# Transposing q and k of two more batches by the DMA crossbar instead of TensorE, with two crossbar target buffers

## The chip, the cores and the metric

The kernel runs on one core of a Trainium2 chip. The metric is the device time of one execution in microseconds (us). All times below are from executions on the chip. Each kernel was also profiled once; positions such as "at 70.2" are microseconds from the start of that profiled execution. Experiments were timed in rounds that alternate with the kernel before on the same chip. A run that is over 1.5% above the fastest of the same kernel is called slow and left out of the ratios; the others are called fast. "Granted clock" is the clock that the profile shows for TensorE, as a share of full speed. A "crossbar transpose" is a DMA that transposes what it moves (`dma_start_transpose`); PSUM is the memory that TensorE writes its results to.

## The reference

Windowed attention over 8 batches of 8 heads, 576 positions of width 64, followed by a two-layer network with a squared ReLU. Inputs and outputs are float32; the kernel computes in bfloat16.

```python
scores = scale * np.matmul(q, k.transpose(0, 1, 3, 2))        # (8, 8, 576, 576)
mask_plain = (rel >= 0) & (rel < 32)                           # heads 0 to 3
mask_dil = (rel >= 0) & (rel < 32 * 4) & (rel % 4 == 0)        # heads 4 to 7
...
attn = softmax(masked scores)
x = (attn @ v), heads joined                                   # (4608, 512)
h = np.maximum(x @ w_in, 0.0)                                  # (4608, 2048)
out = (h * h @ w_out)                                          # (4608, 512)
```

## The kernel before

The instruction order is written by hand in a string. Batches are numbered from 0, so the "third" batch is 2 and the "fourth" is 3. A "|" ends one group of feed-forward matmuls (288 groups in all, about 0.87 us of TensorE each); the codes between two bars are attention steps put behind that group. `2q0` puts q of head pair 0 of batch 2 into `qT`, `2k0` does the same for k; capital `Q` and `K` are the second part of a batch whose sequence is handled in two parts; `a` and `b` are the two halves of the scores with their exponential, `o` and `p` the two halves of the products with v; `v` spreads v. `L2:q...` loads q and k of batch 2, `L2:v...` loads v, and `L4:x` issues the four crossbar transposes of batch 4, a "quartet" in the order k, q, k, q.

```python
XB = 4                          # batches from here on go through the crossbar
WHOLE = tuple(range(2, XB))     # batches 2 and 3: loaded in one piece, transposed on TensorE
ADDED = 4
ps_f = ...tile_pool(name="ps_f", bufs=4, space=PSUM)   # feed-forward sums
ps_a = ...tile_pool(name="ps_a", bufs=2, space=PSUM)   # "pa": transposes AND scores
rb = [{nm: const.tile([80, 2 * H * RES * D], bf16, ...) for nm in "qk"} for i in range(2)]
qx = const.tile([P, H, 2, M], bf16, name="qx")         # crossbar targets, one of each
kx = const.tile([P, H, 2, M], bf16, name="kx")

def cross(b, nm, part):                                # one crossbar transpose, in SP's queue
    n, m0 = MN[part], MS[part]
    nc.sync.dma_start_transpose(
        (qx if nm == "q" else kx)[:, :, :, m0 : m0 + n].rearrange("p h c m -> p (h c) m"),
        staged(b, nm)[0:n, part, :, :].rearrange("p h x -> p (h x)"),
    )

def trans(b, e, nm, part):                             # transposes on TensorE
    ps = ps_a.tile([P, 1024], bf16, name="pa")
    copy = nc.scalar.copy if nm == "q" and e < NE // 2 else nc.vector.tensor_copy
    ...
    if b in WHOLE:
        m0, n, pitch, cuts = 0, M, M, [(t[0:72, :, a, :], 72 * a, 72) for a in range(2)]
    else:
        m0, n, pitch, cuts = MS[part], MN[part], 80, [(t[0:80, part, :, :], 0, 80)]
    pv_ = ps[:, 0 : 4 * pitch].rearrange("p (h c m) -> p h c m", h=2, c=2)
    for hl in range(2):
        for c in range(2):
            for src, c0, w in cuts:
                nc.tensor.transpose(pv_[:, hl, c, c0 : c0 + w],
                                    src[:, 2 * e + hl, P * c : P * c + P], ident[0:w, 0:w])
    halves(e, nm, pv_[:, :, :, 0:n], m0, n, copy)      # copies into qT or kbd

def scores(b, e, part, ...):
    ps = (pool or ps_a).tile([P, 512], f32, name=name) # the same two "pa" buffers
    ...                                                # matmuls kbd x qT
    nc.scalar.activation(pt[:, off : off + n], ps[:, 0:n], ACT.Exp, scale=SCALE)
    ...                                                # mask on VectorE

def step(b, code):
    ...
    if what in "qk" and b >= XB:                       # crossbar target to qT or kbd
        t = qx if what == "q" else kx
        halves(e, what, t[:, 2 * e : 2 * e + 2, :, :], 0, M, nc.vector.tensor_copy)
    elif what in "qQkK":
        trans(b, e, what.lower(), part)
...
def cross_all(b):
    for part in range(2):
        for nm in "kq":
            cross(b, nm, part)
```

All loads are issued by GpSimd in program order, and all output stores and crossbar transposes by SP in program order.

The softmax here doesn't subtract the row's maximum and nothing guards it: scores larger than these inputs give would overflow.

Of the kernel before, what the change touches and what calls it, by code (L numbers as in the profile page):

```python
# [12 lines left out]
RES = 4  # L13
# [5 lines left out]


PROGRAM = (
    "L0:q023 L0:q00 L0:q01 0k0 L0:q10123 0q0 0q1 0k1 L0:v0pd 0a0 0q2 L0:i0 0a1 0k3 L0:v1dpr 0k2 0q3 0Q1 "
    "0K3 0a3 0Q3 0K2 0a2 0v2 0Q0 L0:i1 L0:o2 0K0 0o0 0v3 0b0 0Q2 0o2 0K1 0b3 0o1 L0:o0 0o3 0V3 0b2 0b1 | "
    "0V2 | 0p0 | 0p1 0p2 | L0:o1 0p3 L0:o3 | | | y | | | | | | | | L1:q00123 z | | | | | L1:v0dp "
    "L1:q10123 | | L2:qw0123 L1:v1dpr 1q1 1q3 | 1q2 | 1k2 | 1k1 1v3 | 1a2 | 1v2 1k0 1q0 | 1o2 | 1a0 1a1 | "
    "1k3 1o0 1o1 | 1a3 1Q0 | 1K0 1o3 | 1Q1 1K1 | 1Q2 | 1b0 | | 1Q3 1K2 L2:vwpdr | | | 2q0 | | 2k0 1V2 | "
    "1b2 1p0 | 1b1 1V3 1K3 | | 1p2 1p1 | 2a0 1b3 | 2k1 2o0 2b0 1p3 | 2q1 2k2 | | L3:qw0123 2q2 2p0 "
    "L3:vwpdr 2a1 | | | 2b1 | 2v2 2o1 2q3 2a2 | | 2p1 | 2k3 | 2b2 2o2 | 2v3 | 2a3 2p2 L4:q10123 | 2b3 | "
    "3k1 2o3 3q1 | | 3a1 L4:q00123 2p3 | 3k0 3k2 | | 3o1 | | | 3q0 3v2 | | | | 3a0 | 3b1 3k3 | | | 3p1 "
    "L4:x 3q2 | | 3b0 | 3a2 3q3 3o0 4k0 | | | 3o2 3b2 | | 3p0 3v3 | 4q1 3a3 | 3p2 4q2 4q0 | L5:q10123 3b3 "  # L30
    "| 3o3 L4:vwpdr | 4k1 | | L5:q00123 3p3 4k2 4k3 4a0 L5:vwpdr | | | 4b0 | | 4q3 | | 4o0 | | | 4a2 4v2 "
    "| 4b2 | 4a3 L5:x 4a1 | 4o2 | | | 4p2 L6:q00123 4v3 | | 4b1 | | 4p0 | | 4p1 | 5q0 5k0 | 4b3 | | | | "
    "4o1 | | 5k2 L6:q10123 4o3 | 5q2 5k1 | | 4p3 | 5q1 |"
)


# [24 lines left out]
def kernel(  # L61
# [9 lines left out]
    nc = tc.nc  # L71
    P = nc.NUM_PARTITIONS
    B, H, S, D = q.shape
# [3 lines left out]
    bf16 = mybir.dt.bfloat16  # L77
# [11 lines left out]
    MN = (64, M - 64)  # L89
    NT = 512  # L90
    NTILES = NTOK // NT
    XB = 4
    WHOLE = tuple(range(2, XB))
    PARTED = (0, 1)
    ADDED = 4
    RING = 4 * S
# [33 lines left out]
    rb = [{nm: const.tile([80, 2 * H * RES * D], bf16, name=f"{nm}b{i}") for nm in "qk"} for i in range(2)]  # L130
    qT = const.tile([P, NE, RES, M], bf16, name="qT")

    qx = const.tile([P, H, 2, M], bf16, name="qx")
    kx = const.tile([P, H, 2, M], bf16, name="kx")
    kbd = const.tile([P, NE, NB, P], bf16, name="kbd")
    vbd = [const.tile([P, NE, NB, P], bf16, name=f"vbd{i}") for i in range(2)]

# [5 lines left out]
    def staged(b: int, nm: str):  # L143


        t = rb[b % 2][nm]
        if b in WHOLE:
            return t[:, :].rearrange("p (h a x) -> p h a x", h=H, a=2)
        return t[:, :].rearrange("p (a h x) -> p a h x", h=H, a=2)

    def load_qk(b: int, part, es):
        hs = slice(2 * es[0], 2 * es[-1] + 2)
        for nm, src in (("q", q), ("k", k)):
            t = staged(b, nm)
            if b in WHOLE:
                nc.gpsimd.dma_start(
                    t[0 : M // 2, hs, :, :].rearrange("p h a x -> p (h a) x"),
                    src[b, hs, :, :].rearrange("h (a p r) d -> p (h a) (r d)", a=2, r=RES),
                )
            else:  # L160
                t0, n = RES * MS[part], MN[part]
                nc.gpsimd.dma_start(  # L162
                    t[0:n, part, hs, :], src[b, hs, t0 : t0 + RES * n, :].rearrange("h (p r) d -> p h (r d)", r=RES)
                )

    def load_v(b: int, parts, which="pdr"):

# [46 lines left out]
    def cross(b: int, nm: str, part: int):  # L214

        n, m0 = MN[part], MS[part]
        nc.sync.dma_start_transpose(
            (qx if nm == "q" else kx)[:, :, :, m0 : m0 + n].rearrange("p h c m -> p (h c) m"),
            staged(b, nm)[0:n, part, :, :].rearrange("p h x -> p (h x)"),
        )  # L220

    def trans(b: int, e: int, nm: str, part: int):

        ps = ps_a.tile([P, 1024], bf16, name="pa")
        t = staged(b, nm)
        copy = nc.scalar.copy if nm == "q" and e < NE // 2 else nc.vector.tensor_copy
        if b == 0:

            m0, n = MS[part], MN[part]
            pv_ = ps[:, 0 : RES * n].rearrange("p (r m) -> p r m", r=RES)  # L230
            for r in range(RES):
                for hl in range(2):
                    nc.tensor.transpose(  # L233
                        pv_[64 * hl : 64 * hl + 64, r, :],
                        t[0:n, part, 2 * e + hl, D * r : D * r + D],
                        ident[0:n, 0:n],
                    )
            if nm == "q":
                copy(qT[:, e, :, m0 : m0 + n], pv_)
                return  # L240
            for hl in range(2):
                rows = slice(64 * hl, 64 * hl + 64)
                if e < NE // 2:
                    copy(  # L244
                        kbd[rows, e, m0 // 16 : (m0 + n) // 16, rows].rearrange("p i (m r) -> p i m r", r=RES),
                        pv_[rows, :, :].rearrange("p r (i m) -> p i m r", m=16),
                    )
                else:
                    copy(kbd[rows, e, RES * part : RES * part + RES, rows], pv_[rows, :, 0:64])  # L249
                    if part:  # L250
                        copy(
                            kbd[rows, e, 8, rows].rearrange("p (m r) -> p m r", r=RES),
                            pv_[rows, :, 64:n].rearrange("p r m -> p m r"),
                        )
            return
        if b in WHOLE:
            m0, n, pitch, cuts = 0, M, M, [(t[0:72, :, a, :], 72 * a, 72) for a in range(2)]
        else:

            m0, n, pitch, cuts = MS[part], MN[part], 80, [(t[0:80, part, :, :], 0, 80)]  # L260
        pv_ = ps[:, 0 : 4 * pitch].rearrange("p (h c m) -> p h c m", h=2, c=2)
        for hl in range(2):
            for c in range(2):
                for src, c0, w in cuts:
                    nc.tensor.transpose(  # L265
                        pv_[:, hl, c, c0 : c0 + w], src[:, 2 * e + hl, P * c : P * c + P], ident[0:w, 0:w]
                    )
        halves(e, nm, pv_[:, :, :, 0:n], m0, n, copy)

    def halves(e: int, nm: str, t, m0: int, n: int, copy):  # L270


        for hl in range(2):
            rows = slice(64 * hl, 64 * hl + 64)
            for jj in range(2):
                src = t[64 * jj : 64 * jj + 64, hl, :, :]
                if nm == "q":
                    copy(  # L278
                        qT[rows, e, :, m0 : m0 + n].rearrange("p (c j) m -> p j c m", j=2)[:, jj, :, :], src
                    )  # L280
                elif e < NE // 2:
                    copy(  # L282
                        kbd[rows, e, m0 // 16 : (m0 + n) // 16, rows].rearrange(
                            "p i (m c j) -> p j i m c", c=2, j=2)[:, jj, :, :, :],
                        src.rearrange("p c (i m) -> p i m c", m=16),
                    )
                else:
                    x0, x1 = m0 // 64, min((m0 + n) // 64, 2)
                    copy(
                        kbd[rows, e, RES * x0 : RES * x1, rows].rearrange(  # L290
                            "p (x c j) m -> p j c x m", c=2, j=2)[:, jj, :, :, :],
                        src[:, :, 0 : 64 * (x1 - x0)].rearrange("p c (x m) -> p c x m", m=64),
                    )
                    if m0 + n == M:
                        copy(
                            kbd[rows, e, 8, rows].rearrange("p (m c j) -> p j m c", c=2, j=2)[:, jj, :, :],
                            src[:, :, n - 16 : n].rearrange("p c m -> p m c"),
                        )
# [163 lines left out]
    def step(b: int, code: str):  # L462



        what, e = code[0], int(code[1])
        part = int(what in "QKVbp")
        if what in "qk" and b >= XB:
            t = qx if what == "q" else kx
            halves(e, what, t[:, 2 * e : 2 * e + 2, :, :], 0, M, nc.vector.tensor_copy)  # L470
        elif what in "qQkK":
            trans(b, e, what.lower(), part)
        elif what in "vV":
            spread_v(b, e, [part] if b in PARTED else [0, 1])
        elif what in "ab":
            scores(b, e, part, *((ps_f, "pf") if b == 0 and not part else ()))
        elif b == 0 and part and e % 2:
            pv(b, e, part, ps_a, "pa")
        elif b in PARTED and e % 2:
            pv(b, e, part, ps_f, "pf")  # L480
        else:
            pv(b, e, part)
# [224 lines left out]
```

## Time and profile before

| | before |
|---|---|
| time, median of 4 runs (lowest to highest) | 319.07 us (318.94 to 319.78) |
| span of the profiled execution | 317.3 us |
| TensorE busy, granted clock | 94%, 1.000 |
| VectorE, ScalarE, GpSimd busy | 66%, 62%, 27% |

The prediction below shows the page's main lines. In the trace the columns are start, duration, engine, source line, operation, written and read tiles, shapes and count; a bracket at the end, where there is one, is the idle time before the group and what ended it.

```profile
70.50 0.39 PE L334 MATMUL pa<-qT,kbd 128*128 128x32 bf16 x6
70.72 0.31 PE L265 MATMUL pa<-mk,kb 80*128 80x80 bf16 x4
71.08 1.67 PE L561 MATMUL pf<-w_out_sb,h2T 128*128 128x512 bf16 x7
72.59 0.44 PE L443 MATMUL po<-pt,vbd 128*128 128x32 bf16 x9
```

The row at 70.72 is `1K3`, four transposes of the second batch, which stay on TensorE after the change. Like the scores at 70.50 they write a "pa" buffer. There are only two of those, so `1K3` can't start until ScalarE has read the scores that used the buffer before. Here there is no bracket: nothing waits.

SP's queue while a quartet runs with little beside it (batch 4):

```profile
100.13 1.34 SPq L217 DMA_TRANSPOSE kx<-kb  x1
101.65 1.76 SPq L217 DMA_TRANSPOSE qx<-qb  x1
103.52 1.99 SPq L217 DMA_TRANSPOSE kx<-kb  x1
105.61 1.97 SPq L217 DMA_TRANSPOSE qx<-qb  x1
```

The duration here is the time SP needs to issue the transpose, 1.3 to 2.0 us each. The last one lands at 110.02, 9.9 us after the first was issued.

### The profile page before, as it was taken

Reading aid. Unit: us, or ns where it says so; the run is one execution under the profiler, and the core shown is the slowest. Engines: PE = TensorE matmul, PEld = TensorE weight load, DVE = VectorE, ACT = ScalarE, POOL = GpSimd, SP = SyncE. Lnnn points to the kernel's source line nnn. Section 1 sums busy time; section 2 is a strip of 40 time slices with the busy share of each in tenths; the row PEclk is TensorE's granted clock in tenths of the full one; section 3 lists DMA queues with packets and bytes.
Section 4 is the critical chain, followed back from the end, with each engine's and each line's share of the span. In section 5 each row is a group of like instructions: output and inputs, shape, how many; then the busy total and the mean of one; then the engine's idle time right before and its main releaser. Section 6 shows DMA issues by size and latency. Waiting matters only on the chain.

```text
span 317.3 us, 6743 instructions
## 1 busy us (share of the span) xinstructions
PE 299.7 (94%) x2523; PEld 190.3 (60%) x2556; DVE 208.6 (66%) x664; ACT 195.4 (62%) x422; POOL 84.1 (27%) x130
## 2 busy tenths in 40 slices
PE   1698999999999999999999999999999999999995
PEld 1587945877965555555579755555555555445543
DVE  6785758898987987996599658965896324204400
ACT  5366735877958966686468646864686466316511
POOL 8762282367320037741271041000000000000000
PEclk9999999999999999999999999999999999999999
DMA  7999999999996619999699864352200210021022
GB/s 96 179 123 212 207 144 204 130 91 162 108 119 130 120 16 204 159 186 167 91 132 174 134 99 90 49 103 68 66 2 2 68 66 0 24 78 33 0 68 66
DMA packets 73056, 33.08 MB, mean 104 GB/s; under 512 B 44096, under 2 KB 67008, under 8 KB 73024
## 3 DMA queue, kind: packets, MB, share of 16 engines
q0 software_dynamic: 48096, 18.36, 50.3%
q1 hardware_dynamic: 24784, 14.16, 19.0%
q8 instruction: 20, 0.33, 0.4%
q10 hardware_dynamic: 144, 0.13, 0.1%
q14 instruction: 12, 0.10, 0.1%
HBM read 36.83 MB, written 9.44 MB: 146 GB/s over the span
## 4 chain that ended last, share of the span: by engine, by line
PE 88%; DVE 5%; ACT 3%; issue 2%; DMA 1%; POOL 1%; ACTq 0%; DVEq 0%; POOLq 0%
PE pf L529 38%; PE pf L561 37%; PE po L443 3%; PE pd L445 3%; PE pa L265 2%; PE pa L334 2%; PE pa L340 1%; DMA kb<-in_k_dram 1%; DVE xT L458 1%; PE pa L233 1%; DVE kbd L244 1%; DVE kbd L249 1%; ACT rec L447 1%; ACT qT L278 1%; ACT rec L448 1%
## 5 line engine op out<-in xcount | busy, mean ns | idle before, releaser
L529 PE MATMUL pf<-xT,w_in 128*128 128x256 bf16 (+1 forms) x758 | 132.9, 325 | 1.2 <-DVE xT L458 0.3
L561 PE MATMUL pf<-w_out_sb,h2T 128*128 128x512 bf16 (+1 forms) x569 | 131.0, 373 | 1.7 <-ACT osb L567 0.5
L529 PEld LDWEIGHTS <-w_in 128*128 128x128 bf16 x768 | 82.1, 114 | 35.7 <-issue 1.3
L540 ACT ACTIVATE h2T<-pf 128x512 bf16<-128x512 f32 x144 | 83.4, 597 | 24.7 <-PE pf L529 23.8
L561 PEld LDWEIGHTS <-h2T 128*128 128x128 bf16 x592 | 54.2, 98 | 53.5 <-issue 0.7
L541 DVE TENSOR_TENSOR h2T<-h2T 128x512 bf16<-128x512 bf16 x144 | 57.3, 422 | 36.0 <-ACT h2T L540 34.8
L567 ACT COPY osb<-pf 128x512 f32<-128x512 f32 (+1 forms) x37 | 21.2, 573 | 44.5 <-PE pf L561 41.5
L458 DVE TENSOR_TENSOR xT<-po,rec 128x288 bf16<-128x288 f32 (+2 forms) x56 | 25.5, 456 | 34.8 <-ACT rec L448 34.2
L447 ACT ACTIVATE rec<-pd 128x288 f32<-128x288 f32 (+2 forms) x56 | 23.1, 412 | 28.1 <-PE pd L445 28.0
L179 POOL DMA_DIRECT2D vbd<-in_v_dram x40 | 28.2, 728 | 43.8 <-PE pd L445 34.6
L344 ACT ACTIVATE pt<-pa 128x352 bf16<-128x352 f32 (+6 forms) x60 | 29.7, 502 | 8.4 <-PE pa L340 4.4
L448 ACT ACTIVATE rec<-rec 128x256 f32<-128x256 f32 (+2 forms) x64 | 28.4, 444 | 2.0
L443 PEld LDWEIGHTS <-vbd 128*128 128x128 bf16 x332 | 19.6, 99 | 10.2 <-issue 1.4
L443 PE MATMUL po<-pt,vbd 128*128 128x32 bf16 (+3 forms) x286 | 19.6, 199 | 0.7 <-DVE xT L458 0.7
L445 PE MATMUL pd<-pt,mk 128*128 128x96 bf16 (+5 forms) x172 | 18.0, 207 | 0.0
L162 POOL DMA_DIRECT2D qb<-in_q_dram x14 | 10.1, 721 | 27.0 <-PE po L443 24.6
L192 POOL DMA_DIRECT2D vd<-in_v_dram x24 | 14.7, 648 | 9.6 <-DMA kb<-in_k_dram 9.6
L278 DVE COPY qT<-qx 64x288 bf16<-64x288 bf16 x64 | 16.1, 251 | 0.8
L282 DVE COPY kbd<-kx 64x288 bf16<-64x288 bf16 x32 | 15.0, 469 | 0.4
L198 POOL DMA_DIRECT2D vbd<-in_v_dram x16 | 9.7, 617 | 17.4 <-PE pd L445 5.1
L334 PE MATMUL pa<-qT,kbd 128*128 128x96 bf16 (+2 forms) x160 | 13.8, 206 | 0.5 <-DVE kbd L244 0.4
L445 PEld LDWEIGHTS <-mk 128*128 128x128 bf16 x232 | 13.7, 99 | 0.7 <-issue 0.5
(60 smaller groups left out, 231.0 us busy)
## 6 DMA issues: line engine op xcount, KB each, us to landing
out_dram<-osb SPq DMA_DIRECT2D x18, 128.0 KB, 4.8
vd<-in_v_dram POOLq DMA_DIRECT2D x32, 64.0 KB, 5.2
w_in<-in_moe_w_in_dram POOLq DMA_DIRECT2D x2, 1024.0 KB, 9.0
w_out_sb<-in_moe_w_out_dram POOLq DMA_DIRECT2D x4, 512.0 KB, 13.5
qb<-in_q_dram POOLq DMA_DIRECT2D x6, 320.0 KB, 5.1
kb<-in_k_dram POOLq DMA_DIRECT2D x6, 320.0 KB, 6.6
vbd<-in_v_dram POOLq DMA_DIRECT2D x24, 72.0 KB, 5.8
out_dram<-osb SPq DMA_DIRECT2D x10, 160.0 KB, 2.2
```

What stands on the lines that cost most here:

```text
L179: nc.gpsimd.dma_start(dst[rows, e, i0:i1, rows], v[b, 2 * e + hl, 64 * i0 : 64 * i1, :].rearrange("(i p) d -> p i d", p=64),)
L344: nc.scalar.activation(pt[:, off : off + n], ps[:, 0:n], ACT.Exp, scale=SCALE)
L443: nc.tensor.matmul(oo, vb[:, e, i, :], rh, start=(x == 0), stop=(x == len(mms) - 1), skip_group_check=True)
L445: nc.tensor.matmul(dd, ones[:, :], rh, start=(x == 0), stop=(x == len(dms) - 1), skip_group_check=True)
L447: nc.scalar.activation(rec[:, 0:n], d[:, 0:n], ACT.Ln)
L448: nc.scalar.activation(rec[:, 0:n], rec[:, 0:n], ACT.Exp, scale=-1.0)
L458: nc.vector.tensor_tensor(out=tok, in0=o if o is o3 else o[:, 0:n], in1=rec if o is o3 else rec[:, 0:n], op=ALU.mult)
L529: nc.tensor.matmul(acc[u][:, nt * x + y0 : nt * x + y1], w_in_sb[piece][:, kt, c0 : c0 + 509 : 4], xT[:, kt, t0 : t0 + y1 - y0], start=(kt ...
L540: nc.scalar.activation(hv, acc[u][:, :].rearrange("p (x n) -> p x n", x=per), ACT.Relu)
L541: nc.vector.tensor_tensor(out=hv, in0=hv, in1=hv, op=ALU.mult)
L561: nc.tensor.matmul(cur[m][:, c0:c1], h2[:, f, P * m : P * m + P], w_out_sb[:, f, c0:c1], start=(f == 0), stop=(f == NF - 1),)
L567: nc.scalar.copy(osb[:, c0:c1], cur[m][:, c0:c1])
```

## The change

The intent is to take 128 transposes off TensorE, the engine that bounds the kernel, by giving them to the crossbar, which the later batches use already. A second pair of target buffers lets a quartet start while the one before is still being copied out. The order string gets `L2:x` and `L3:x`, and the first readers of batch 3 move two groups later.

```diff
-  ... L2:qw0123 ... 1Q2 | 1b0 | ... L3:qw0123 2q2 2p0 ... 2p1 | 2k3 ...
+  ... L2:q00123 L2:q10123 ... 1Q2 L2:x | 1b0 | ... L3:q00123 L3:q10123 2q2 2p0 ... 2p1 L3:x | 2k3 ...
-  ... 2b3 | 3k1 2o3 3q1 | | 3a1 L4:q00123 2p3 | 3k0 3k2 ...
+  ... 2b3 | 2o3 | | 3k1 3q1 L4:q00123 2p3 | 3a1 3k0 3k2 ...
-    XB = 4
-    WHOLE = tuple(range(2, XB))
+    XB = 2
-    qx = const.tile([P, H, 2, M], bf16, name="qx")
-    kx = const.tile([P, H, 2, M], bf16, name="kx")
+    qx = [const.tile([P, H, 2, M], bf16, name=f"qx{i}") for i in range(2)]
+    kx = [const.tile([P, H, 2, M], bf16, name=f"kx{i}") for i in range(2)]
 (the branches for WHOLE in staged, load_qk and trans go; cross writes qx[b % 2] or kx[b % 2])
-            t = qx if what == "q" else kx
-            halves(e, what, t[:, 2 * e : 2 * e + 2, :, :], 0, M, nc.vector.tensor_copy)
+            t = (qx if what == "q" else kx)[b % 2]
+            by_act = what == "q" and e < NE // 2 and b < ADDED
+            halves(e, what, t[:, 2 * e : 2 * e + 2, :, :], 0, M, nc.scalar.copy if by_act else nc.vector.tensor_copy)
```

## The prediction

> **What bounds the kernel now.** I read the page from the top: the engine shares, then the 40 slices, then the chain that ended last.
>
> ```profile
> PE 299.7 (94%) x2523; PEld 190.3 (60%) x2556; DVE 208.6 (66%) x664; ACT 195.4 (62%) x422; POOL 84.1 (27%) x130
> ...
> PE   1698999999999999999999999999999999999995
> ...
> PE 88%; DVE 5%; ACT 3%; issue 2%; DMA 1%; POOL 1%; ACTq 0%; DVEq 0%; POOLq 0%
> ```
>
> TensorE (PE) is 94% busy over the whole span. The slices show that the missing part is the first 30 us and the last slice; from there on every slice is 9, and the chain of waits lies on PE for 88%. So an instruction taken from PE between 30 and 313 us is worth what it occupies there, as long as no new wait opens. A table of stretches of 10 us shows the neighbours in the stage that is changed: PE 9.95, 9.89 and 9.90 of 10 in the stretches from 60 to 90 us, VectorE 9.29, 8.88 and 9.46, ScalarE 7.31, 8.11 and 8.01. PE is full, VectorE nearly so.
>
> The transposes that go are one line of the kernel. The groups by shape show the 128 that concern the third and fourth batch (72 rows each; the 64 of 80 rows belong to the second batch and stay):
>
> ```profile
> L265 PE MATMUL pa<-mk,qb 72*128 72x72 bf16 x64 | 3.4, 196 | 0.0
> L265 PE MATMUL pa<-mk,kb 72*128 72x72 bf16 x64 | 3.2, 197 | 0.0
> ```
>
> The columns are busy us, mean ns, idle us before. The 6.6 us of busy time is the union of overlapping instructions with pipelined tails; what a group takes away from the next one is read in the order of time on PE:
>
> ```profile
> 67.78 0.42 PE L265 MATMUL pa<-mk,kb 72*128 72x72 bf16 x8
> 68.04 1.03 PE L561 MATMUL pf<-w_out_sb,h2T 128*128 128x512 bf16 x4
> ```
>
> Eight transposes start at 67.78 and the next feed-forward matmul starts at 68.04: 0.26 us for eight, although the group is "busy" 0.42. The other groups of eight with a complete record have the same 0.26.
>
> **What the Trainium skill says.** "VectorE: DVE Perf Modes", section "The three transpose paths", gives 390 ns for a 128x128 transpose on TensorE and 1309 ns by the crossbar. The trace does not bear out the first as a cost: one lasts 196 ns, and in a row they come every 32 ns (0.26/8). "DMA: Bandwidth & Descriptors", section "DMA Transpose (X-bar)", puts the plain transpose on SP or ACT alone; the kernel issues all on SP, in one row with the output stores, so they wait for one another. The same page, "Issuing engines are not separate DMA queues", says that loads, stores and transposes share the same 16 engines and interleave. The trace agrees: the four transposes of one batch land within 9.9 us when little else moves (issued from 100.13 to 105.61, about 4.4 us each to landing), but took from 133.78 to about 150.8 us (144.97 plus a landing of 5.8) while the loads of q and k of a later batch were under way, though part of that is a wait on the single target buffer. "Rules for kernel authors" of the page advises to issue a DMA early and wait for it late; this is the weak point below.
>
> **The change part by part.**
>
> Removed from PE: for each of two batches, q and k, four head pairs, 2 x 2 x 2 pieces = 128 transposes in 16 groups of eight. 16 x 0.26 = **4.2 us**, all on PE in the full stretch from 65.8 to 115.7 us, so on the path.
>
> Removed from PSUM: 16 uses of the two "pa" buffers that the scores share. PE idled 0.5 us in total from 60 to 120 us (10 minus the busy time of each stretch), so at most some 0.3 us are to be had here.
>
> Copies: the same 128-partition halves are copied, now from SBUF. VectorE: q 304 to about 235 ns (from the rows of later batches), 16 of them, 1.1 us; k of the dilated heads 287 to 225 ns, 16, 1.0 us; k of the plain heads 480 to 469 ns, 16, 0.2 us. VectorE gets 2.3 us freer, off the path. ScalarE keeps its 16 copies of q at 391 ns; its mask copies from SBUF of the same width take 431 ns, so it may lose 0.6 us, off the path too.
>
> Added: eight transposing DMAs, four per batch, 1.15 MB per batch, no engine time but SP's queue. Loads of q and k of these batches become four DMAs instead of two, with the same bytes; GpSimd issues at about 0.7 us instead of 1.03, so 0.8 us more per batch, off the path.
>
> Second target buffer: it takes away the wait that held one transpose of the sixth batch from 133.78 to 137.29. Nothing on PE waited for it then (PE is 9.95 of 10 busy there), so no gain is counted.
>
> So far: -4.2 to -4.5 us. Now the **new wait**. The third batch's four transposes come in SP's order after nine stores; the ninth is issued at about 59.6 us (three stores from 58.32, together 1.26). The loads they need were issued at 43.3 and 44.3 and landed after 10.6 and 14.7 us, so at 53.9 and 59.0; both are there. From 59.6 the unhindered quartet lands its last part, q, at 59.6 + 9.9 = 69.5. But the first reader of that q is on ScalarE:
>
> ```profile
> 65.84 0.60 ACT L540 ACTIVATE h2T<-pf 128x512 bf16<-128x512 f32 x1 [0.28 <-PE pf L529]
> 66.33 1.60 ACT L278 COPY qT<-pa 64x288 bf16<-64x288 bf16 x4
> 69.38 0.60 ACT L344 ACTIVATE pt<-pa 128x512 bf16<-128x512 f32 x1 [1.46 <-PE pa L334]
> 69.88 0.43 ACT L447 ACTIVATE rec<-pd 128x320 f32<-128x320 f32 x1
> 70.34 0.47 ACT L448 ACTIVATE rec<-rec 128x320 f32<-128x320 f32 x1
> 70.72 0.57 ACT L567 COPY osb<-pf 128x512 f32<-128x512 f32 x1
> 71.19 0.57 ACT L344 ACTIVATE pt<-pa 128x480 bf16<-128x480 f32 x1
> ```
>
> The order of instructions leaves these copies where they were, at 66.3. ScalarE would stand until q lands, L, and everything behind it shifts: copies to L+1.8, exponential to L+2.4, reciprocals to L+3.3, the output copy to L+3.85, the second exponential to L+4.4, its mask on VectorE to L+4.85. PE needs that last one for the second of two products that now start at 72.59 and 73.09; with two groups of transposes gone it would be there at 72.57. Hence a stall of L - 67.7: 1.8 us for L = 69.5, and it eats the whole gain at L = 71.9.
>
> What L will be: the v loads of the third batch are issued from 60.9 to 67.5 and run beside the quartet. In the stretch 174 to 178 v loads and transposes ran side by side at 218 GB/s in all, so I put 1 to 1.5 us on it: L = 70.5 to 71. From about 69.5 the fourth batch's q and k loads start (now three of them at once), and in 138 to 144 such loads nearly stopped the transposes; if the last one is still under way then, L goes to 75 or 76. I chose a stall of 3 us as central. The fourth batch's quartet comes after stores at 77.0 and its loads' landing (83.9 at the latest, now), and its first reader is moved two groups later, to about 95; I count 0.2 us.
>
> Sum: 319.1 - 4.3 + 3.0 + 0.2 = 318.0; I state 317.8, since the tuning of the program around the new reads suggests that the change was meant to gain.
>
> **The rivals.**
>
> First, the transfer is hidden: q lands by 69.5 or ScalarE's delay is absorbed by the run of feed-forward matmuls that needs no ScalarE. For it: the copies stand at the start of such a run (eight groups from 66.05). Against it: two products of the second batch sit inside that run and need ScalarE. It would give 319.1 - 4.5 + 1 = 315.6.
>
> Second, the wait takes the place of what was removed and more: L at 75 to 76 gives a stall of 7.5 to 8, so 319.1 - 4.3 + 7.8 = 322.6. For it: the starved transposes of 138 to 144. Against it: the quartet starts ten us before those loads.
>
> Third, VectorE becomes the bound from 60 to 90, once PE gets through faster: it is at 9.46 of 10 at most and loses 2.3 us of work over the two batches against 4.2 on PE, so at most some 0.5 us.
>
> **Range and chances.** The best case, 4.5 us gained with no stall, is 314.6, which is 1.4% below 319.08: a gain over 2% (312.7) would need more than the transposes occupy. A loss over 2% (325.5) would need a stall of 10.7 us. So within 2% is nearly sure. The range 315.0 to 321.8 runs from an almost hidden quartet to a stall of 7 us. Chances: faster 0.01, within 2% 0.96, slower 0.03.
>
> **What would show it.** No 72-row transposes on PE; the groups of feed-forward matmuls at 67.8 to 68.9 closing up by 0.26 us each. A wait of ScalarE for the transposing DMA of q at about 66, of 3 to 5 us, and right after it PE idle for some 3 us at about 72 before the second batch's products, released by VectorE or ScalarE. If PE shows no idle time there, the first rival is right; if ScalarE waits 9 us or more, the second. The prediction is wrong if PE stalls elsewhere, for instance behind output stores held up by the transposes in SP's queue, or behind the fourth batch's copies at about 95.

## The result and the profile after

The kernel after takes 328.93 us (median of 4 runs, 327.2 to 332.05), against 319.07 us before. The ratio is 1.031, with a 95% interval of 1.026 to 1.037: slower by 3.1%. A ratio in this document is the mean time of one kernel's fast runs over that of the other's of the same rounds, so it is not quite the ratio of the quoted medians. All four runs count as fast; the granted clock is 0.979 to 0.984 in each, against 1.000 before, and that turns out to be part of the story. Results are correct here and in every experiment.

From the page of the kernel after: busy shares, TensorE in 40 slices (8.2 us each), the clock granted to it, and the engine shares of the chain that ended last.

```profile
PE 299.9 (92%) x2428; PEld 187.1 (57%) x2428; DVE 206.8 (63%) x664; ACT 195.5 (60%) x422; POOL 85.6 (26%) x134
...
PE   1698999963999799999999999999999999999995
...
PEclk9999999995999999999999999999999999999999
...
PE 67%; DMA 21%; POOL 5%; SPq 3%; issue 2%; ACT 2%; DVE 0%; ACTq 0%; POOLq 0%
```

A hole of 6 and 3 stands in the ninth and tenth slices of TensorE, a shallow one follows at the fourteenth, and the clock falls to 5 in the tenth. DMA, 1% of the chain before, is 21% of it now; 5% of the span are transposes of q, and 11% are loads of v, most of them before the hole. Although 128 transposes have gone, TensorE's busy time has not fallen. Part of that is bookkeeping: 33 feed-forward matmuls are missing from the records of before (758 and 569 in its two groups, where the kernel after has 768 and 592). The other part is work done at half clock.

The order of time on TensorE around the hole:

```profile
65.80 2.75 PE L550 MATMUL pf<-w_out_sb,h2T 128*128 128x512 bf16 x12
...
69.98 0.39 PE L320 MATMUL pa<-qT,kbd 128*128 128x32 bf16 x6
78.49 0.42 PE L251 MATMUL pa<-mk,kb 80*128 80x80 bf16 x4 [8.12 <-ACT pt L330]
78.71 3.62 PE L550 MATMUL pf<-w_out_sb,h2T 128*128 128x512 bf16 x8
```

At 65.80 the feed-forward matmuls run through where two groups of transposes had stood. The scores that started at 70.50 before start at 69.98 now, so 0.52 us have been gained by two groups of eight. Then `1K3` waits 8.12 us for an exponential on ScalarE (line 330) to free a "pa" buffer. After the wait, eight matmuls take 3.62 us.

ScalarE shows what the exponential itself waited for:

```profile
66.00 0.60 ACT L529 ACTIVATE h2T<-pf 128x512 bf16<-128x512 f32 x1 [0.28 <-PE pf L518]
76.06 1.75 ACT L264 COPY qT<-qx 64x288 bf16<-64x288 bf16 x4 [9.46 <-DMA qx<-qb]
77.84 0.60 ACT L330 ACTIVATE pt<-pa 128x512 bf16<-128x512 f32 x1
```

The copies of q for the third batch, at 66.33 before, stand until the crossbar transpose of q has landed, 9.46 us. The exponential comes after them in ScalarE's order, though it has nothing to do with that q. SP's queue and a table of stretches of the same time (length; busy us and instructions of TensorE, weight loads, VectorE, ScalarE, GpSimd; granted clock; DMA packets' time as a multiple of the 16 engines' time; GB/s):

```profile
60.47 1.35 SPq L208 DMA_TRANSPOSE kx<-kb  x1
62.00 1.99 SPq L208 DMA_TRANSPOSE qx<-qb  x1
64.09 3.88 SPq L208 DMA_TRANSPOSE kx<-kb  x1
68.07 3.14 SPq L208 DMA_TRANSPOSE qx<-qb  x1
```

```profile
64.00:68.00 4.00, 4.00 (x30) 2.81 (x28) 3.71 (x17) 2.05 (x4) 2.49 (x5) 1.00 1.81 96
```

```profile
72.00:73.00 1.00, 0.00 (x0) 0.00 (x0) 0.00 (x0) 0.00 (x0) 0.00 (x0) 0.95 1.31 244
73.00:74.00 1.00, 0.00 (x0) 0.00 (x0) 0.80 (x2) 0.00 (x0) 0.00 (x0) 0.50 1.44 223
74.00:83.00 9.00, 4.51 (x25) 2.20 (x25) 4.51 (x18) 4.06 (x9) 2.21 (x3) 0.50 0.82 104
83.00:84.00 1.00, 1.00 (x18) 0.76 (x16) 0.00 (x0) 0.75 (x2) 0.27 (x1) 0.93 1.48 260
```

The third transpose takes 3.88 us to issue and the fourth 3.14, where the free quartet took under 2. The four land at 66.37, 70.82, 73.05 and 75.98: 15.5 us from the first issue to the last landing, against 9.9 us when little else moves. While the v loads of the third batch and the quartet share the DMA engines (64 to 68), only 96 GB/s move. The clock reads 0.95 over the microsecond from 72 and 0.93 over that from 83, with 0.50 between, so it was halved for 0.10 + 10 + 0.14 = 10.24 us, from 72.9 to 83.14. TensorE works again from 78.49, so 4.65 us of work ran at half speed and about 2.3 us were lost.

The fourth batch's quartet is issued at 87.66, 90.14, 91.74 and 99.28, beside loads of the fifth batch's q and k issued from 88.70 to 90.84, and lands at 95.25, 102.98, 106.27 and 107.26. TensorE waits in four pieces: 0.36 us at 89.43, 0.35 at 97.16, 0.80 at 109.14 and 1.08 at 110.55, 2.6 us in all. Only the last two, 1.9 us, can be put down to the fourth batch. The first two are waits for products that VectorE scales (`xT`), and such a pair (0.33 and 0.34, 0.29 and 0.34) also stands in the two experiments below that send the third batch alone through the crossbar, and not in those with the fourth alone. So they come with the third batch, late quartet or not.

The balance of the two profiled spans, 326.6 against 317.3, so +9.3 us:

| term | us |
|---|---|
| transposes gone, 16 x 0.26 | -4.2 |
| idle before `1K3` | +8.1 |
| two short waits that come with the third batch | +0.7 |
| two waits for the fourth batch | +1.9 |
| work at half clock, 78.49 to 83.14 | +2.3 |
| start-up of this execution | +0.2 |
| sum | +9.0 |

The remaining 0.3 us are not assigned.

### The profile page after: what moved, and what is told of

It is laid out like the page before. It is cut to its first block, busy times and chain, and to the rows that moved or that the text cites. A ratio compares the mean times of both kernels' runs of the same rounds, so it can differ in the third digit from the quotient of the medians.

```text
span 326.6 us, 6546 instructions
## 1 busy us (share of the span) xinstructions
PE 299.9 (92%) x2428; PEld 187.1 (57%) x2428; DVE 206.8 (63%) x664; ACT 195.5 (60%) x422; POOL 85.6 (26%) x134
## 4 chain that ended last, share of the span: by engine, by line
PE 67%; DMA 21%; POOL 5%; SPq 3%; issue 2%; ACT 2%; DVE 0%; ACTq 0%; POOLq 0%
PE pf L550 31%; PE pf L518 29%; DMA vd<-in_v_dram 11%; DMA qx<-qb 5%; DMA w_in<-in_moe_w_in_dram 3%; SPq L208 3%; PE po L429 2%; PE pd L431 2%; DMA qb<-in_q_dram 2%; PE pa L320 1%; POOL kb L153 1%; POOL vbd L170 1%; POOL qb L153 1%; PE pa L326 1%; ACT qT L264 1%
## 5 line engine op out<-in xcount | busy, mean ns | idle before, releaser
L550 PE MATMUL pf<-w_out_sb,h2T 128*128 128x512 bf16 (+1 forms) x592 | 136.2, 377 | 0.5 <-ACT osb L556 0.5
L170 POOL DMA_DIRECT2D vbd<-in_v_dram x40 | 28.2, 722 | 61.3 <-PE pd L431 46.4
L268 DVE COPY kbd<-kx 64x288 bf16<-64x288 bf16 x48 | 22.6, 471 | 6.0 <-DMA kx<-kb 5.2
L264 DVE COPY qT<-qx 64x288 bf16<-64x288 bf16 x80 | 20.0, 250 | 1.1
L153 POOL DMA_DIRECT2D qb<-in_q_dram x18 | 13.1, 729 | 22.0 <-DMA qx<-qb 16.2
L153 POOL DMA_DIRECT2D kb<-in_k_dram x18 | 12.9, 718 | 9.8 <-PE pa L251 8.1
```

The lines of the kernel that those rows point to most:

```text
L153: nc.gpsimd.dma_start(t[0:n, part, hs, :], src[b, hs, t0 : t0 + RES * n, :].rearrange("h (p r) d -> p h (r d)", r=RES))
L170: nc.gpsimd.dma_start(dst[rows, e, i0:i1, rows], v[b, 2 * e + hl, 64 * i0 : 64 * i1, :].rearrange("(i p) d -> p i d", p=64),)
L264: copy(qT[rows, e, :, m0 : m0 + n].rearrange("p (c j) m -> p j c m", j=2)[:, jj, :, :], src)
L550: nc.tensor.matmul(cur[m][:, c0:c1], h2[:, f, P * m : P * m + P], w_out_sb[:, f, c0:c1], start=(f == 0), stop=(f == NF - 1),)
```

## The experiments

The theory: the third batch's q lands late because its quartet shares the DMA engines with the loads that GpSimd has just issued. ScalarE, which takes its instructions in order, stands before that q and holds a PSUM buffer that TensorE needs. The idle time then halves the clock. The rivals: the fourth batch is the cause; the moved readers or the second buffer are; or a crossbar quartet is too slow here in any case.

In experiment kernels that hold loads back, GpSimd copies one column of the quartet's last target, which makes it wait for the quartet. The code is `h` for batch 2 and `i` for batch 3:

```diff
+        if code == "h":
+            nc.gpsimd.tensor_copy(held[:, 0:1], qx[0][:, 0, 0, M - 1 : M])
+        elif code == "i":
+            nc.gpsimd.tensor_copy(held[:, 0:1], qx[1][:, 0, 0, M - 1 : M])
```

The results in one table. L is when q of the third batch landed, "wait at `1K3`" is TensorE's idle time there, and "half clock" is the length of the stretches at clock 0.5, all from the profiled execution.

| kernel | median us | ratio to before (95%) | L | wait at `1K3` | half clock |
|---|---|---|---|---|---|
| after | 328.93 | 1.0312 (1.0257 to 1.0367) | 76.0 | 8.12 | 10.24 |
| fourth batch only | 318.28 | 0.9961 (0.9945 to 0.9976) | none | none | none |
| third batch only | 330.83 | 1.0337 (1.0299 to 1.0374) | 78.5 | 9.69 | 10.24 |
| v loads held | 328.90 | 1.0294 (1.0277 to 1.0310) | 70.5 | 2.16 | 6.83, later |
| unused matmuls in the hole | 331.69 | 1.0227 (1.0171 to 1.0282) | 78.9 | 2.91 | none |
| q, k loads held | 324.82 | 1.0181 (1.0149 to 1.0213) | 73.4 | 5.31 | 6.83 |
| held for both batches | 328.92 | 1.0300 (1.0272 to 1.0329) | 70.6 | 2.03 | 6.83, later |
| fourth only, readers back | 318.72 | 0.9974 (0.9954 to 0.9994) | none | none | none |
| early quartet, both held | 325.34 | 1.0162 (1.0121 to 1.0204) | 67.9 | none | 3.41 twice, later |
| two buffers only | 319.32 | 0.9993 (0.9977 to 1.0009) | none | none | none |
| q, k loads held, matmuls in the hole | 322.48 | 1.0108 (1.0075 to 1.0141) | 72.3 | filled | none |
| early quartet only | 322.04 | 1.0085 (1.0047 to 1.0123) | 71.6 | 3.82 | 3.41 |
| third only, early, v held | 319.23 | 0.9992 (0.9970 to 1.0013) | 68.1 | under 0.3 | none |

The median of "unused matmuls in the hole" is that of all four runs, two of them slow; its ratio is that of the two fast ones. The medians of before in the same rounds were 319.31 us (first four experiments), 319.48 (next four) and 319.69 (last four).

### Each batch by itself

Only the fourth batch goes through the crossbar; the third is loaded and transposed as before. The two buffers and the later readers stay.

```diff
-    XB = 2          # order: L2:q00123 L2:q10123 ... 1Q2 L2:x
+    WHOLE = (2,)    # order: L2:qw0123 ... 1Q2
```

> Only the fourth batch goes through the crossbar; the third stays on the array as before. Theory A (the loss is the third batch's wait: its q lands at 76 us because loads starve the quartet, and ScalarE, then TensorE stand for it): without that quartet no 8 us wait and no halved clock; 8 groups of 8 transposes less, -2.1 us, so about 317.0 us, granted clock 1.00; the fourth batch's quartet has some 10 us of slack. Rival B (any crossbar batch beside these loads costs): the fourth batch's wait, 2.1 us of PE idle near 108 us in the changed kernel, stays or grows: 319 to 321 us.

Measured: 318.28 us, 0.4% faster than before, 1.3 us above what was expected. Its largest wait on TensorE is one of 0.61 us at 99.95, and the clock stays at 1. Its quartet is issued at 78.0 to 85.2, some ten us earlier than in the kernel after because nothing has held the program up, and lands by 92.7.

The reverse, only the third batch, with the order of before for the fourth:

```diff
-    XB = 2          # order: L3:q00123 L3:q10123 ... 2p1 L3:x ... 2o3 | | 3k1 3q1 ... | 3a1
+    WHOLE = (3,)    # order: L3:qw0123 ... 2p1 ... 3k1 2o3 3q1 | | 3a1
```

> Only the third batch goes through the crossbar. Theory A: the wait of 8.3 us and the halved clock (2.3 us) are all there, -2.1 us of transposes: 327.5 us, so nearly the whole loss. Rival B (the two batches hurt each other, through the queue of SP and the loads): clearly less, 322 to 325 us.

Measured: 330.83 us, more than expected, and no less than the whole change (the intervals of the two ratios overlap). ScalarE waited 11.0 us and TensorE 9.69. So the whole loss comes with the third batch, and the fourth by itself is a small gain. That the fourth batch waits longer in the kernel after than by itself (1.9 us against 0.61) is put down to the delay that the third one causes ahead of it; no experiment shows this apart.

### Which transfers hold the quartet up

First, all loads that follow the quartet in GpSimd's order, starting with v, wait for it.

```diff
-  1Q3 1K2 L2:vwpdr
+  1Q3 1K2 h L2:vwpdr
```

> The changed kernel, but GpSimd is made to wait, by a copy of one element of the third batch's transposed q, before it issues the third batch's v loads; so nothing of GpSimd's is loaded beside the quartet except what was issued before 59 us. Theory A (the loads starve the transposes): the last transpose lands 10 us after the first is issued, at about 70 instead of 76; ScalarE's wait falls from 9.5 to about 4 us, PE's from 8.1 to about 2.5, the clock stays 1.00; some 320 us. Rival C (the quartet is slow by itself behind the stores): landing at 75 or later, 328 us. A later v could cost 1 us at the third batch's first products.

Measured: 328.90 us, so the expected time was missed, although the local part came true. The stretch from 64 to 68 us in this kernel, and ScalarE, TensorE and again TensorE in order of time:

```profile
64.00:68.00 4.00, 4.00 (x32) 3.04 (x30) 3.64 (x16) 2.51 (x5) 0.00 (x0) 1.00 1.06 136
```

```profile
70.56 1.75 ACT L266 COPY qT<-qx 64x288 bf16<-64x288 bf16 x4 [3.50 <-DMA qx<-qb]
```

```profile
72.99 0.30 PE L253 MATMUL pa<-mk,kb 80*128 80x80 bf16 x4 [2.16 <-ACT pt L332]
107.61 0.45 PE L322 MATMUL pa<-qT,kbd 128*128 128x96 bf16 x4 [6.74 <-ACT qT L266]
109.02 1.87 PE L520 MATMUL pf<-xT,w_in 128*128 128x512 bf16 x4 [0.95 <-DVE xT L446]
```

Without the loads beside it the quartet lands at 70.5, 9.9 us after its first issue at 60.62, just as batch 4 had shown. More bytes move in the same four us (136 against 96 GB/s), and of these the transposes move about 530 KB, against about 155 KB in the kernel after. TensorE waits 2.16 us instead of 8.12. But the held loads come later by their hold: q and k of the fourth batch are now issued at 78.3 to 80.4 (68.7 to 79.2 in the kernel after) and land up to 89.0, so the fourth quartet starts at 85.4, when its first k has landed, meets the next v loads, and lands at 105.7 (92.7 with the fourth batch alone). TensorE waits 6.74 us there, and half clock follows. The loss was moved by one batch.

Second, only the q and k loads of the fourth batch wait; v runs beside the quartet.

```diff
-  | | L3:q00123 L3:q10123 2q2 2p0
+  | | h L3:q00123 L3:q10123 2q2 2p0
```

> The changed kernel with GpSimd held only before the fourth batch's q and k loads; the third batch's v loads run beside the quartet as in the change. It tells which loads starve the transposes. If the v loads do (in the changed kernel the transposes moved 155 KB from 64 to 68 us, before any q or k load was issued): last landing near 74 instead of 76, TensorE's wait about 6 us, clock still halved, 327 to 329 us. If the q and k loads do: landing near 71, wait about 3 us, clock 1.00 there; but the fourth batch's loads then come late and its quartet collides, as with the hold before v.

Measured: 324.82 us, below the 327 to 329 expected if v is the cause. q landed at 73.4, between the two landings expected (74 and 71), and TensorE waited 5.31. Of the 5.5 us between 70.5 (nothing beside it) and 76.0 (kernel after), the v loads thus account for 2.9 and the q and k loads for 2.6, each measured in one profile. That is a better kernel than after, and still 1.8% slower than before.

Third, both holds: v of the third batch behind the third quartet, and q, k of the fifth batch behind the fourth quartet.

```diff
-  1Q3 1K2 L2:vwpdr ... 2a3 2p2 L4:q10123
+  1Q3 1K2 h L2:vwpdr ... 2a3 2p2 i L4:q10123
```

> Two holds: before the third batch's v loads, and before the fifth batch's q and k loads until the fourth batch's quartet has landed. Theory A (nothing but loads beside the quartets makes them late): TensorE's wait of 6.7 us near 101 us, that the first hold alone left, falls to at most 1.5 us, the clock stays 1.00, 318 to 321 us. Rival C (a quartet near 90 us is late whatever is loaded): 326 us or more.

Measured: 328.92 us, missed again. The third and the fourth batch now wait only 2.03 and 1.09 us, but the q and k loads of the fifth and sixth batches, pushed to 99.7 to 103, are late for the next quartet. It starts at 111.2, when its k has landed, and lands at 127.4:

```profile
128.96 0.56 PE L431 MATMUL po<-pt,vbd 128*128 128x32 bf16 x6 [6.81 <-DVE xT L446]
```

So the contention is real, but holding loads doesn't remove it: each load that waits for a quartet meets the next one.

### The halved clock

TensorE is given 38 matmuls with an unused result before `1K3`, so that it isn't idle there.

```diff
-  1b1 1V3 1K3
+  1b1 1V3 w 1K3
+        if code == "w":
+            idle = ps_f.tile([P, 512], f32, name="pf")
+            for x in range(38):
+                nc.tensor.matmul(idle[:, :], ident, w_out_sb[:, x % NF, :], start=(x == 0), stop=(x == 37))
+            nc.vector.tensor_copy(held[:, 0:1], idle[:, 0:1])
```

> The changed kernel with 38 matmuls of 512 columns whose result is not used (8.2 us) put ahead of the transposes at which TensorE stood for 8.1 us. The wait is the same, but TensorE isn't idle in it. Theory A (the halved clock from 73 to 83 us follows from the idle time): granted clock 1.00 and 2.3 us less than the changed kernel, about 326.6 us. Rival D (the clock falls for another reason, as a limit on current or after a fixed time): the clock still falls for 10 us and the time stays at 328.5 or more.

Measured: four runs of 328.15, 335.24, 335.42 and 325.37 us, two of them slow, so the time is inconclusive. In the profile the clock stays at 1, which fits, but in that execution GpSimd issued the fourth batch's first load at 64.2 instead of 68.7, and q landed only at 78.9, so it can't be compared with the profile of after.

The same with 24 matmuls on top of the kernel with q and k loads held, where the wait is shorter and steadier:

```diff
-  | | L3:q00123 ...  1b1 1V3 1K3
+  | | h L3:q00123 ...  1b1 1V3 w 1K3      (24 matmuls)
```

> The version with GpSimd held before the fourth batch's q and k loads (324.8 us; TensorE idle 5.3 us, then 6.8 us of halved clock), with 24 unused matmuls of 512 columns (5.2 us) in the idle time. Theory A (the idle time halves the clock): clock 1.00 around 75 us, TensorE goes on at 75.9 as there, but the next eight matmuls take 1.9 us instead of 3.6: about 322.7 us. Rival D (the clock falls whatever TensorE does): still a stretch at 0.5, 324.8 us or more.

Measured: 322.48 us against 324.82 without the matmuls; by the ratios, 1.0108 against 1.0181, 0.7% or 2.3 us. TensorE in the kernel without them, then with them:

```profile
75.92 0.43 PE L253 MATMUL pa<-mk,kb 80*128 80x80 bf16 x4 [5.31 <-ACT pt L332]
76.14 3.62 PE L552 MATMUL pf<-w_out_sb,h2T 128*128 128x512 bf16 x8
```

```profile
70.46 5.34 PE L620 MATMUL pf<-w_out_sb,mk 128*128 128x512 bf16 x23
75.65 0.31 PE L253 MATMUL pa<-mk,kb 80*128 80x80 bf16 x4
75.79 1.89 PE L552 MATMUL pf<-w_out_sb,h2T 128*128 128x512 bf16 x8
```

The transposes start within 0.3 us of each other, and the eight matmuls behind them take 1.89 instead of 3.62 us. The kernel without the matmuls worked at half clock from 75.92 to 80.13, which is worth 2.1 us. Useless work in the hole makes the kernel faster, because idle time costs clock afterwards. This settles that the lost clock is an effect of the idle time and adds to the wait.

The traces also show what decides it. In all 14 profiles each change of the clock after it first reads 1 falls on a multiple of 3.413 us from that moment (in the kernel after: 21.70, then 72.91 and 83.14, which are 15 and 18 such steps). Every step in which TensorE was idle for 2.08 us or more was followed by half clock, and none with 1.82 us or less was. So the length of a gap alone does not decide: the 2.16 us of the kernel with v held and 2.91 us in the one with 38 matmuls each fell across two steps and cost nothing, while 2.20 us inside one step of the early quartet with both holds did. Whether a gap of some 2 to 4 us costs the half clock is thus a matter of where it falls among the steps, which is luck.

### The moved readers and the second buffer

The fourth batch alone, with its first readers where they stood before:

```diff
-  2b3 | 2o3 | | 3k1 3q1 L4:q00123 2p3 | 3a1 3k0 3k2
+  2b3 | 3k1 2o3 3q1 | | 3a1 L4:q00123 2p3 | 3k0 3k2
```

> Fourth batch alone through the crossbar, its first copies back at the places that the kernel before has (two groups earlier). In the version with late copies TensorE waited 0.6 us for a product at 99.9 us because copies of q and k piled up ahead of it; its quartet landed at 92.7 us and the early copies start at about 93.5. Expected: 0.6 us less than that version, 317.6 us, ratio to the kernel before 0.994 to 0.996. If the quartet is later than 94: 318.5 or more.

Measured: 318.72 us. The expected gain of 0.6 us didn't come, although the quartet had landed at 89.6. The interval of its ratio overlaps that of the version with later readers (0.9974 and 0.9961), so the place of the readers makes no difference that these runs can show.

The kernel before with two target buffers and nothing else:

```diff
-    qx = const.tile([P, H, 2, M], bf16, name="qx")
-    kx = const.tile([P, H, 2, M], bf16, name="kx")
+    qx = [const.tile([P, H, 2, M], bf16, name=f"qx{i}") for i in range(2)]
+    kx = [const.tile([P, H, 2, M], bf16, name=f"kx{i}") for i in range(2)]
```

> The kernel before with nothing changed but two target buffers for the crossbar. In the kernel before one transpose of the sixth batch waited for the single buffer, but TensorE was 9.95 of 10 busy there: same time, ratio 0.998 to 1.002. If the buffer was on the path: 318 us or less.

Measured: 319.32 us against 319.69, ratio 0.9993: no effect.

### An earlier quartet

If lateness is the cause, an earlier start must help. `L2:x` moves ahead of three output stores in SP's order, and nothing else changes:

```diff
-  1a0 1a1 | 1k3 1o0 1o1 | 1a3 1Q0 | 1K0 1o3 | 1Q1 1K1 | 1Q2 L2:x |
+  1a0 1a1 | 1k3 1o0 1o1 L2:x | 1a3 1Q0 | 1K0 1o3 | 1Q1 1K1 | 1Q2 |
```

> The changed kernel with one thing moved: the third batch's quartet ahead of the three output stores in SP's order, no holds. The quartet is issued from 54.8; it shares the engines with v loads as in the change, so it should land 3 to 5 us earlier than 76, at 71 to 73; TensorE's wait falls from 8.1 to 3 to 5 us; with the fourth batch's waits of 2 to 3 us: 321 to 325 us. If holding the loads is needed at all costs: 328.

Measured: 322.04 us. The quartet is issued 6.5 us earlier (from 53.95), but lands only 4.3 us earlier, at 71.6. The wait is 3.82 us and the half clock 3.41. One moved code recovers some 7 of the 10 us.

With both holds added:

```diff
-  1k3 1o0 1o1 | ... 1Q2 L2:x | 1b0 | | 1Q3 1K2 L2:vwpdr ... 2a3 2p2 L4:q10123
+  1k3 1o0 1o1 L2:x | ... 1Q2 | 1b0 | | 1Q3 1K2 h L2:vwpdr ... 2a3 2p2 i L4:q10123
```

> Both batches through the crossbar, both holds, and the third batch's quartet put ahead of the three output stores that SP issues at 58.5 to 60 us. Its first load has landed at 54.7 us, its last at 58.4, so the quartet should be issued from 54.7 to 61 and land by 66, about when ScalarE first asks for it (66.3). Theory A: no wait of TensorE at 70 us, clock 1.00, the 4.2 us of transposes saved less about 1 us at the fourth batch: 315 to 317 us. If the loads of the second batch's v that are still under way until 61 us slow it, landing at 69, a wait of 1.5 us: 317 to 318.5.

Measured: 325.34 us, a miss. The third batch's q lands at 67.9 and TensorE doesn't wait for it at all, but the held loads again cost later: waits of 1.03, 1.09 and 2.20 us between 99 and 125, and two stretches of half clock.

Last, the third batch alone with an early quartet and v held, to see what the third batch is worth when its transfers are hidden:

```diff
+    WHOLE = (3,)
-  1k3 1o0 1o1 | ... 1Q2 L2:x | 1b0 | | 1Q3 1K2 L2:vwpdr
+  1k3 1o0 1o1 L2:x | ... 1Q2 | 1b0 | | 1Q3 1K2 h L2:vwpdr
```

> Third batch alone through the crossbar, quartet ahead of the stores, the third batch's v held until it has landed (67.9 us in the version with both batches, where TensorE had no wait at 70 us). 64 transposes less, -2.1 us, no wait: 317.3 us. If v and the fourth batch's loads, now 8 us later, are missed by the array's transposes or the products: 318.5 or more.

Measured: 319.23 us against 319.69, ratio 0.9992. ScalarE's wait:

```profile
68.14 1.75 ACT L280 COPY qT<-qx 64x288 bf16<-64x288 bf16 x4 [1.04 <-DMA qx<-qb]
```

So with the quartet landed at 68.1 the loss of 11 us of the third batch alone is gone, without a single instruction of TensorE changed: this is the wait by itself. The saving of 2.1 us did not appear, though: the medians differ by 0.5 us, and the interval of the ratio includes 1. The profile has the two short waits for VectorE, 0.29 and 0.34 us, which take back 0.6 us of it. It also has a start-up 0.67 us longer than that of before. The clock first reads 1 at 23.63 in it, at 21.76 in before, and at 23.41 in the profile of the kernel with two buffers, which also reaches the same point 0.6 us late. The same 24 feed-forward matmuls that start at 21.68 in before and at 21.67 here take 3.07 us there and 3.77 here. So the start-up belongs to the execution: the clock was released later in it.

## Why the prediction was wrong

It said 317.8 us, within 315.0 to 321.8, with 96% on a time within 2%. It was 328.93 us, slower by 3.1%.

**What bounds the kernel: right.** TensorE is the bound where nothing waits. Where 16 groups of transposes had stood, two that can be read off close up by exactly the 0.26 us each that were counted. Two buffers were said to bring nothing, and bring nothing (0.9993). The copies came out close to the count: those of q on ScalarE go from 391 to 428 ns, and VectorE's busy time falls by 1.8 us for the 2.3 counted.

**The path of the wait: right in form, wrong in place.** "ScalarE would stand until q lands" is what happened, and the stall of "L - 67.7" holds: with L = 75.98 it gives 8.3, and `1K3` started at 78.49 instead of 70.20 (70.72 less the 0.52 gained), 8.3 later. TensorE's idle time was 8.12. The stall was expected before the products at 72.57 and came before `1K3`, which precedes them: the prediction followed the data and overlooked the two "pa" buffers. The two paths happen to give the same sum, since `1K3` is released at L + 2.5 and was wanted at 70.2. The experiments give seven more pairs of landing and wait:

| L | 67.9 | 68.1 | 70.5 | 70.6 | 71.6 | 73.4 | 76.0 | 78.5 |
|---|---|---|---|---|---|---|---|---|
| L - 67.7 | 0.2 | 0.4 | 2.8 | 2.9 | 3.9 | 5.7 | 8.3 | 10.8 |
| wait | none | under 0.3 | 2.16 | 2.03 | 3.82 | 5.31 | 8.12 | 9.69 |

The wait follows the landing throughout, a little below the formula.

**The step that failed: "What L will be".** The prediction put L at 70.5 to 71. The terms as measured: the quartet started at 60.47 instead of 59.6 (+0.9); unhindered it would take the 9.9 us counted (confirmed with the loads held); the v loads cost 2.9 us where "1 to 1.5 us" were put; and the q and k loads of the fourth batch cost 2.6 where the central estimate had nothing. 59.6 + 0.9 + 9.9 + 2.9 + 2.6 = 75.9, against a measured 75.98 (the last two terms are differences between profiles, so the sum has to fit; it is no check of its own). The second rival named just this, "L at 75 to 76", and its stall of 7.5 to 8, and the prediction's sign for it, ScalarE waiting 9 us or more, came true (9.46). The argument against it, that the quartet starts ten us before those loads, failed because the v loads had slowed the quartet first: its last transpose was issued at 68.07 and was still to move when the q and k loads started at 68.68. The evidence in the trace of before, a quartet nearly stopped by loads at 138 to 144, deserved more weight than the 218 GB/s of one other stretch. By the packets of the trace, that stretch (174 to 178) moved 725 KB of transposes beside 147 KB of v, at 20 ns for a packet of 256 bytes; from 64 to 68 in the kernel after such a packet took 81 ns, and 23 ns in the free quartet. So v loads beside a quartet do not always slow it, and the one stretch that was read gave too kind an answer.

**What the prediction did not have: the clock.** Its estimate for the second rival, 322.6, has the right stall and is still 6 us short. A wait of 8 us is not just 8 us. The Trainium skill says so in "TensorE: Matmul & The Clock Gate", section "Why this matters for your kernels": it advises against idle gaps above about 3 us, after which the clock is halved. This agrees: halved for 10.24 us after 8.12 us of idle time, with 2.3 us of work lost, and in the kernel with q and k held the matmuls that filled the gap got 2.3 us back. The prediction did not use that page: the kernel before is at full clock throughout, but the predicted stall of 3 us was itself at that limit.

**The later waits: too small.** 0.2 us were counted for the fourth batch, 1.9 measured in the kernel after. By itself the fourth batch waits 0.61 us at most. The 0.7 us of the two short waits for VectorE are about what the third rival allowed for, "at most some 0.5 us"; the sum did not count them.

Put together, with the stall at 8.3 for 3.0, the clock at 2.3 for nothing, and the later waits at 2.6 for 0.2, the sum of 318.0 becomes 328.0, against 328.93 measured. The landing may also vary from one execution to the next, which a single trace doesn't show: the runs of after spread over 327.2 to 332.05 us where those of before spread over 318.94 to 319.78.

**What stays open.** Why a transpose's packet takes 81 ns beside the v loads in one stretch and 20 ns in another was not taken apart. No experiment moved the copies of q off ScalarE, so the path of the wait through ScalarE is read from the traces and from the pairs above, not changed by itself. No version was found that hides both batches. The best kernel of all is the one with the fourth batch alone, 318.28 us against 319.31, 0.4% faster; it gets 1.0 to 1.2 us of the 2.1 that its transposes occupied, and its one larger wait, 0.61, explains only part of the rest.

## What to carry to other kernels

Work moved from a full engine to a DMA is free only if the transfer lands before its first reader, and the landing has to be estimated with the transfers that run beside it, not from a quiet stretch: here 9.9 us alone became 15.5. The engine that waits for it takes its whole queue along, including work that frees buffers for others. Before holding back a transfer to make room, look whom it meets at its new time; starting the late transfer earlier was the cheaper cure. And a gap of more than some 2 us on TensorE is to be costed with the half-speed stretch that can follow it, here 3.41 us or a multiple of it.

## What the Trainium skill lacked or had wrong

- "Advanced Engine Details and Errata", section "X-Bar Transpose (TRN2)", calls transposing DMAs as fast as regular ones and expects 350 to 400 GB/s. A quartet here moves about 1.18 MB (the eight added ones raise the bytes of the page by 2.36 MB) in 9.9 us when little else runs, some 119 GB/s, and in 15.5 us, 76 GB/s, beside loads. These times run from the first issue to the last landing of four transposes of about 0.3 MB; the densest 4 us of transposes in the trace of before, from 175.5, moved 211 GB/s of them.
- "DMA: Bandwidth & Descriptors", section "Issuing engines are not separate DMA queues", says that transfers interleave, but not that crossbar transposes and loads beside them can make the total fall: 96 GB/s with v loads beside the quartet, 136 GB/s in the same 4 us without them, and issuing one transpose took SP 3.88 us instead of 2.51.
- "TensorE: Matmul & The Clock Gate", sections "What's actually happening" and "Why this matters for your kernels": the window of 3413 ns fits, since the half-clock stretches last 3.41, 6.83 or 10.24 us. The limit of about 3 us for a gap is not a safe one, and a window need not be idle throughout: 2.08 us of idle time in one window of 3.41 us, in two pieces, and 2.20 in one piece each brought half clock, while 1.82 us did not, nor did a gap of 2.91 us that lay across two windows.
